# Attention, then a mixture of experts: tokens go by rank to a region per expert, and the experts run as a list of tiles

## The chip, the cores and the metric

The kernel runs on one core of one Trainium2 chip. The core has five engines with queues of their own: PE (TensorE, matrix products; its weight loads are listed apart as PEld), DVE (VectorE), ACT (ScalarE), POOL (GpSimd) and SP (SyncE, here only an issuer of DMAs). All work is in float32. The metric is the device time of one execution in microseconds (us); less is better.

## The reference, cut to what matters

```python
# 1. chunked attention: B=4, H=8, S=768, D=64; chunks of 32, each sees 16 keys to its left, 8 to its right, 8 memory keys
a = exp(scores - max);  a = a / (sum(a) + 1e-9);  out[chunk] = a @ v_full
# 2. x = out as (B, S, 512); each token goes through ONE of E=8 experts
logits = x @ w_gate                      # (B, S, 8)
local_gate = sigmoid(x @ w_local)
for b in range(B):
    for s in range(S):
        fresh = argmax(logits[b, s])
        e = fresh if s == 0 or local_gate[b, s] < 0.5 else e    # else the expert of the token before
        p = softmax(logits[b, s])
        out[b, s] = p[e] * (relu(x[b, s] @ w1[e]) @ w2[e])      # w1: 512x1024, w2: 1024x512 per expert
```

## The kernel before, in words

`attention` works in 32 blocks of 96 queries, 8 to a batch, 4 to a load ("unit": tiles `qt`, `kt`, `vt`, two buffers each). Per block: `scores`, `values` and `logits`. After the 8 blocks of a batch, `route` computes probabilities and experts. `x`, with 8 probabilities behind each token, goes to `x_dram` in token order with one plain DMA per batch on SP's queue. The row `onehot` of each expert and a running count of its tokens (`cum`) stay on chip.

`experts` starts with a sort. From `cum` each token's slot follows, and from the slots, by 32 + 32 small products, the token of each slot (`idx`) and where its result goes (`put`). Slots form tiles of 128, each tile of one expert; 31 tiles are possible, and `bound` holds where each expert's tiles begin. All 31 tiles are then gathered from `x_dram` by indirect DMAs on POOL's queue, turned by PE (`g_ps`) and kept in `xst`. Last comes, for each expert, a loop with a trip count that is known only on the chip (`For_i_unrolled`, two tiles to a pass) over `product`: 32 matmuls into `h_ps`, Relu into `ht`, 8 matmuls into `y_ps`, a scaling into `y`, and an indirect DMA that puts the rows into `out`. The pool `wp` holds the weights of two experts: those of experts 0 and 1 are loaded by SP during attention, those of expert e + 2 after the loop of expert e. A matmul of float32 stands as two instructions in the profile, a transpose as one.

The tile framework writes the waits, and a scheduler sets the order of instructions within straight-line code; it moves nothing past a branch.

Of the kernel before, what the change touches and what calls it, by code (L numbers as in the profile page):

```python
# [15 lines left out]
P = 128  # L16
# [17 lines left out]
XW = D + E                   # a token's row: x, then its probability for each expert  # L34
NTILE = NT // P + E - 1      # tiles of 128 slots when each expert's tokens begin a tile
# [10 lines left out]
@with_exitstack  # L46
def kernel(
    ctx: ExitStack,
    tc: tile.TileContext,
    q: bass.AP,  # L50
    k: bass.AP,
    v: bass.AP,
    mem_k: bass.AP,
    mem_v: bass.AP,
    w_gate: bass.AP,
    w_local: bass.AP,
    w1: bass.AP,
    w2: bass.AP,
    out: bass.AP,
):  # L60
# [25 lines left out]


@with_exitstack
def attention(ctx, tc, q, k, v, mem_k, mem_v, w_gate, w_local, x_dram, ident, onehot, cum, eidx, load_weights):
    """Chunked attention into x_dram; its tokens' experts into onehot, and their ranks (from 1) into cum."""  # L90
# [45 lines left out]
    def mask_of(qb):  # L136
        return masks["first" if qb == 0 else "last" if qb == NQB - 1 else "mid"]

    # e - 8 for each expert; 8 s + 8 for each token s of a batch
# [4 lines left out]
                   allow_small_or_imprecise_dtypes=True)  # L144

# [47 lines left out]
    def route(b, x, lt):  # L193
        """Probabilities into x; the experts of the batch, each carried on by the tokens that its gate keeps."""
# [5 lines left out]
        ex = sm.tile([QB, NQB, E], F32, name="ex")  # L200
        nc.scalar.activation(ex, below, ACT.Exp)
        tot = sm.tile([QB, NQB, 1], F32, name="tot")
        nc.vector.tensor_reduce(tot, ex, axis=AX.X, op=ALU.add)
        nc.vector.tensor_scalar(tot, tot, 1e-9, None, ALU.add)
        nc.vector.reciprocal(tot, tot)
        nc.vector.tensor_tensor(x[:, :, D:XW], ex, tot.to_broadcast([QB, NQB, E]), op=ALU.mult)
        nc.sync.dma_start(x_dram[S * b:S * b + S].rearrange("(j p) c -> p j c", p=QB), x)

# [26 lines left out]
        seg = slice(S * b, S * b + S)  # L235
        nc.vector.tensor_scalar(onehot[:, seg], expert, eidx, None, ALU.is_equal)
# [23 lines left out]
def experts(ctx, tc, x_dram, out, ident, onehot, cum, load_weights, weights):  # L260
# [4 lines left out]
    idx = once.tile([P, NTILE], I32, name="idx")  # L265
    put = once.tile([P, NTILE], I32, name="put")
    bound = once.tile([1, E + 1], I32, name="bound")

    with tc.tile_pool(name="sort", bufs=1) as so, tc.tile_pool(name="sops", bufs=1, space=PSUM) as sops:
        # before[e, m] = 1 where e < m  # L270
        before = so.tile([E, E + 1], F32, name="before")
# [3 lines left out]
        ones = so.tile([E, 1], F32, name="ones")  # L275
        nc.gpsimd.memset(ones, 1.0)
        lo_no = so.tile([QB, P], F32, name="lo_no")
        nc.gpsimd.iota(lo_no, pattern=[[1, P]], base=0, channel_multiplier=0, allow_small_or_imprecise_dtypes=True)
        token = so.tile([QB, NB, 1], F32, name="token")
        nc.gpsimd.iota(token, pattern=[[QB, NB], [0, 1]], base=1, channel_multiplier=1,  # L280
                       allow_small_or_imprecise_dtypes=True)

        # tiles of each expert, and those before its first
        tiles_i = so.tile([E, 1], I32, name="tiles_i")
        nc.vector.tensor_scalar(tiles_i, cum[:, NT - 1:NT], float(P - 1), None, ALU.add)
        nc.vector.tensor_scalar(tiles_i, tiles_i, 7, None, ALU.logical_shift_right)
        tiles = so.tile([E, 1], F32, name="tiles")
        nc.vector.tensor_copy(tiles, tiles_i)
        b_ps = sops.tile([1, E + 1], F32, name="b_ps")
        nc.tensor.matmul(b_ps, lhsT=tiles, rhs=before, start=True, stop=True)  # L290
        nc.vector.tensor_copy(bound, b_ps)
        t_ps = sops.tile([E, 1], F32, name="t_ps")
        nc.tensor.matmul(t_ps, lhsT=before[:, 0:E], rhs=tiles, start=True, stop=True)
        base = so.tile([E, 1], F32, name="base")
        nc.vector.tensor_scalar(base, t_ps, float(P), -1.0, ALU.mult, ALU.add)

        # each token's slot
        nc.vector.scalar_tensor_tensor(cum, cum, base, onehot, ALU.add, ALU.mult)
        s_ps = sops.tile([QB, NB], F32, name="slot_ps")
        for n in range(NB):  # L300
            nc.tensor.matmul(s_ps[:, n:n + 1], lhsT=cum[:, QB * n:QB * n + QB], rhs=ones, start=True, stop=True)
        slot = so.tile([QB, NB], I32, name="slot")
        nc.vector.tensor_copy(slot, s_ps)
# [116 lines left out]
```

## Time and profile before

| what | value |
|---|---|
| time, median of 3 runs | 944.22 us (941.28 to 945.43) |
| span of the profiled execution | 944.2 us |
| PE busy, PEld busy | 757.7 us (80%), 593.7 us (63%) |
| DVE, ACT, POOL busy | 206.0, 169.2, 61.1 us |
| DMA moved | 78.03 MB, 83 GB/s over the span |
| tiles that ran (out of 31) | 27 (DMAs `out_dram<-y,to`) |

The span of the profiled execution is the time of the median run, so that sums made on the trace need no correction. The span falls into three stages: attention up to the last copy of logits (`lt`, ended at 326.1 us), route of the last batch with sort and gathers up to the first product (425.6 us), and the products. PE's busy share is high in all of them, but the trace also shows at which clock PE ran.

### The profile page before, as it was taken

What the parts mean: (1) busy time and instruction counts of PE and PEld (TensorE: products, weight loads), DVE (VectorE), ACT (ScalarE), POOL (GpSimd) and SP (SyncE); (2) the same over time, 40 slices, a digit from 0 to 9 for tenths busy, and PEclk for the clock granted to TensorE, in tenths of its full rate; (3) what the DMA queues carried; (4) which work ended last, traced back from release to release, by engine and by line L of the source; (5) the groups of instructions that cost most, each with busy time, mean ns of one, the idle gap of its engine ahead of it and who ended that gap; (6) DMA issues with size and microseconds to landing.
All of it is one profiled execution on the core that took longest, in us unless ns stands there. A gap on an engine that the chain in (4) does not pass through costs nothing. (4 is left out here: it accounts for less than half of the span.)

```text
span 944.2 us, 12427 instructions
## 1 busy us (share of the span) xinstructions
PE 757.7 (80%) x4144; PEld 593.7 (63%) x4144; DVE 206.0 (22%) x529; ACT 169.2 (18%) x421; POOL 61.1 (6%) x80
## 2 busy tenths in 40 slices
PE   4979889899898745769798968969769779673978
PEld 3877678687777645448565755746547557442655
DVE  3544644555464342330000000000000000000000
ACT  2523234243243000111010101101101011010110
POOL 0000000000000000650000000000000000000000
PEclk8655555555555555558798979979989889895999
DMA  9792331622120010660002040031023000507000
GB/s 238 260 299 72 117 94 28 188 64 59 27 87 1 22 47 3 198 150 11 11 12 82 36 184 21 14 136 58 11 85 127 11 22 12 190 23 270 9 23 2
DMA packets 44458, 78.03 MB, mean 83 GB/s; under 512 B 20269, under 2 KB 20397, under 8 KB 44400
## 3 DMA queue, kind: packets, MB, share of 16 engines
q1 hardware_dynamic: 33728, 54.10, 17.3%
q0 software_dynamic: 4640, 14.55, 5.1%
q10 hardware_dynamic: 6032, 8.61, 3.5%
q8 instruction: 36, 0.59, 0.3%
q14 instruction: 22, 0.18, 0.1%
HBM read 64.57 MB, written 13.47 MB: 83 GB/s over the span
## 5 line engine op out<-in xcount | busy, mean ns | idle before, releaser
L363 PE MATMUL h_ps<-xst,w_sb 128*128 x1728 | 238.2, 301 | 94.4 <-DVE pe L355 41.3
L363 PEld LDWEIGHTS h_ps<-xst,w_sb 128*128 128x128 f32 x1728 | 228.0, 213 | 119.1 <-issue 105.5
L369 PE MATMUL y_ps<-w_sb,ht 128*128 128x512 f32 x432 | 189.9, 592 | 0.0
L369 PEld LDWEIGHTS y_ps<-w_sb,ht 128*128 128x128 f32 x432 | 80.0, 190 | 90.4 <-issue 90.4
L355 DVE COPY pe<-prob 128x1 f32 x27 | 4.2, 154 | 480.8 <-PEq L379 180.1
L174 PE MATMUL o_ps<-vt,pt 128*96 128x65 f32 x512 | 91.5, 354 | 9.4 <-DVE x L178 5.1
L174 PEld LDWEIGHTS o_ps<-vt,pt 128*96 128x96 f32 x512 | 84.6, 267 | 17.4 <-issue 10.4
L161 ACT ACTIVATE s_sb<-s_sb,nmax 96x128 f32<-96x128 f32 x256 | 80.5, 390 | 31.4 <-DVE nmax L159 31.4
L151 PE MATMUL s_ps<-kt,qt 64*96 64x128 f32 x512 | 76.0, 432 | 12.5 <-DMA kt<-in_k_dram 9.1
L366 ACT ACTIVATE ht<-h_ps 128x512 f32<-128x512 f32 x54 | 32.2, 597 | 298.0 <-PE h_ps L363 298.0
L151 PEld LDWEIGHTS s_ps<-kt,qt 64*96 64x96 f32 x512 | 56.6, 265 | 22.2 <-issue 15.1
L168 PE MATMUL pt_ps<-ident,s_sb 96*128 96x96 f32 x256 | 59.2, 374 | 12.7 <-ACT pt L170 9.0
L372 POOL DMA_INDIRECT out_dram<-y,to x27 | 26.6, 984 | 496.6 <-ACT y L371 431.2
L168 PEld LDWEIGHTS pt_ps<-ident,s_sb 96*128 96x128 f32 x256 | 43.2, 224 | 23.1 <-ACT pt L170 13.8
L170 ACT COPY pt<-pt_ps 128x384 f32<-128x384 f32 x64 | 30.4, 477 | 139.1 <-PE o_ps L174 98.6
L371 ACT ACTIVATE y<-y_ps,pe 128x512 f32<-128x512 f32 x27 | 18.6, 687 | 169.4 <-PE y_ps L369 169.4
L345 PE MATMUL g_ps<-ident,xs 128*128 128x128 f32 x124 | 33.3, 428 | 16.8 <-DMA xs<-x_dram,idx 12.8
L190 PEld LDWEIGHTS l_ps<-wg,xt 128*96 128x96 f32 x256 | 42.2, 265 | 2.2 <-DVE xt L187 0.9
L190 PE MATMUL l_ps<-wg,xt 128*96 128x9 f32 x256 | 41.5, 292 | 0.7 <-DVE xt L187 0.7
L345 PEld LDWEIGHTS g_ps<-ident,xs 128*128 128x128 f32 x124 | 22.2, 217 | 27.6 <-issue 16.7
L159 DVE TENSOR_REDUCE nmax<-s_sb 96x8 f32<-96x1024 f32 x32 | 38.3, 1198 | 0.1
L339 POOL DMA_INDIRECT xs<-x_dram,idx x31 | 29.5, 952 | 51.6 <-issue 41.6
(86 smaller groups left out, 308.8 us busy)
## 6 DMA issues: line engine op xcount, KB each, us to landing
w_sb<-in_w_dram SPq DMA_DIRECT2D x16, 2048.0 KB
vt<-in_v_dram ACTq DMA_DIRECT2D x32, 243.8 KB
kt<-in_k_dram SPq DMA_DIRECT2D x32, 240.0 KB
x_dram<-x SPq DMA_DIRECT2D x4, 1560.0 KB
qt<-in_q_dram SPq DMA_DIRECT2D x8, 768.0 KB
vt<-in_mem_v_dram ACTq DMA_DIRECT2D x32, 16.2 KB
xs<-x_dram,idx POOLq DMA_INDIRECT x31
out_dram<-y,to POOLq DMA_INDIRECT x27
```

The source lines that it names most:

```text
L151: nc.tensor.matmul(s_ps[:, u, a], lhsT=qt[h, a, QB * j:QB * j + QB], rhs=kt[h, j, a], start=True, stop=True)
L159: nc.vector.tensor_reduce(nmax, s_sb, axis=AX.X, op=ALU.max, negate=True)
L161: nc.scalar.activation(s_sb[:, i], s_sb[:, i], ACT.Exp, bias=nmax[:, i:i + 1])
L168: nc.tensor.transpose(pt_ps[:, a], s_sb[:, HP * u + a], identity=ident[:QB, :QB])
L170: nc.scalar.copy(pt, pt_ps)
L174: nc.tensor.matmul(o_ps[:, a], lhsT=pt[:, a], rhs=vt[:, j, VW * h:VW * h + VW], start=True, stop=True)
L190: nc.tensor.matmul(l_ps, lhsT=xt[:, kk], rhs=wg[:, kk], start=(kk == 0), stop=(kk == DK - 1))
L339: nc.gpsimd.indirect_dma_start(out=xs, out_offset=None, in_=x_dram[:, :], in_offset=bass.IndirectOffsetOnAxis(ap=idx[:, i:i + 1], axis=0))
L345: nc.tensor.transpose(g_ps[:, kk], xs[:, P * kk:P * kk + P], identity=ident)
L363: nc.tensor.matmul(h_ps[:, m], lhsT=w1_sb[:, kk, P * (g + m):P * (g + m) + P], rhs=xst[:, bass.ds(i, 1), kk, :].rearrange("p o n -> p (o n)"),
L366: nc.scalar.activation(ht[:, g:g + 4], h_ps, ACT.Relu)
L369: nc.tensor.matmul(y_ps, lhsT=ht[:, m], rhs=w2_sb[:, m], start=(m == 0), stop=(m == FK - 1))
```

## The change

1. `route` ends otherwise. `count` is carried over batches; each token's row in DRAM is `4096 * expert + rank`, computed by one more DVE operation and 8 matmuls (`r_ps`). A row of `x` is now 514 words: 512 of x, the probability of its own expert, the token's number. The 8 blocks of the batch go to these rows by 8 indirect DMAs on POOL's queue (L263 of the kernel after).
2. The sort is gone. A plan for 31 tiles (expert, first row, last row of each) is made from the 8 counts by some 25 small DVE operations.
3. The loops are gone. 24 tiles (3072 tokens / 128, the least there can be) stand in straight-line code, and 7 more each inside an `If(total > i)`, nested. A tile's own loads of `w1` and `w2` (4.2 MB, four buffers each, the expert read from `table`), its gather and its transposes stand in the tile.
4. No weights are loaded during attention. The host lays `w1` and `w2` out so that a partition's share is one run of 16 KB (before: runs of 4 KB and 2 KB).

```diff
-XW = D + E                   # a token's row: x, then its probability for each expert
+XW = D + 2
+SURE = NT // P
+NTILE = SURE + E - 1
+REGION = 4096
+WBUF = 4
@@ route
-        nc.sync.dma_start(x_dram[S * b:S * b + S].rearrange("(j p) c -> p j c", p=QB), x)
...
-        nc.vector.tensor_tensor_scan(cum[:, seg], onehot[:, seg], onehot[:, seg],
-                                     cum[:, S * b - 1:S * b] if b else 0.0, ALU.add, ALU.max)
+        nc.vector.tensor_tensor_scan(rank, onehot, onehot, count, ALU.add, ALU.max)
+        nc.vector.tensor_copy(count, rank[:, S - 1:S])
+        nc.vector.scalar_tensor_tensor(rank, rank, region, onehot, ALU.add, ALU.mult)
+        r_ps = xps.tile([QB, NQB], F32, name="r_ps", tag="xps")
+        for n in range(NQB):
+            nc.tensor.matmul(r_ps[:, n:n + 1], lhsT=rank[:, QB * n:QB * n + QB], rhs=ones, start=True, stop=True)
+        row = sm.tile([QB, NQB], I32, name="row")
+        nc.vector.tensor_copy(row, r_ps)
...
+        nc.vector.tensor_tensor(x[:, :, D:D + 1], mine, tot, op=ALU.mult)
+        nc.vector.tensor_copy(x[:, :, D + 1:XW], token[:, NQB * b:NQB * b + NQB])
+        for n in range(NQB):
+            nc.gpsimd.indirect_dma_start(
+                out=x_dram[:, :], out_offset=bass.IndirectOffsetOnAxis(ap=row[:, n:n + 1], axis=0),
+                in_=x[:, n].bitcast(I32), in_offset=None)
...
-        if 2 <= n < 4:
-            load_weights(n - 2)
@@ experts
-    for i in range(NTILE):
-        xs = gp.tile([P, XW], F32, name="xs")
...
+    def load(i):
+        e = nc.values_load(table[:, i:i + 1], engines=[SP], min_val=0, max_val=E - 1,
+                           skip_runtime_bounds_check_because="made from counts of tokens")
+        xs = gp.tile([P, XW], F32, name="xs")
+        nc.gpsimd.indirect_dma_start(
+            out=xs.bitcast(I32), out_offset=None, in_=x_dram[:, :],
+            in_offset=bass.IndirectOffsetOnAxis(ap=rows[:, i:i + 1], axis=0))
+        w1_sb = wp.tile([P, DK, F], F32, name="w1_sb")
+        nc.sync.dma_start(w1_sb, w1[bass.ds(e, 1)].rearrange("o p k f -> p (o k) f"))
+        w2_sb = wp.tile([P, FK, D], F32, name="w2_sb")
+        nc.sync.dma_start(w2_sb, w2[bass.ds(e, 1)].rearrange("o p m d -> p (o m) d"))
+        return xs, w1_sb, w2_sb
+
+    def turned(i, xs):
         g_ps = gps.tile([P, DK, P], F32, name="g_ps")
         for kk in range(DK):
             nc.tensor.transpose(g_ps[:, kk], xs[:, P * kk:P * kk + P], identity=ident)
...
+        xt = gp.tile([P, DK, P], F32, name="xt")
+        nc.vector.tensor_copy(xt, g_ps)
+        to = hp.tile([P, 1], I32, name="to")
+        nc.vector.tensor_tensor(to, xs[:, D + 1:XW], past[:, i:i + 1], op=ALU.add)
+        return xt, to
...
-    for e in range(E):
-        a, z = (nc.values_load(bound[0:1, n:n + 1], min_val=0, max_val=NTILE,
-                               skip_runtime_bounds_check_because="a count of tiles") for n in (e, e + 1))
-        tc.For_i_unrolled(a, z, 1, lambda i: product(e, i), max_unroll=2)
-        if e + 2 < E:
-            load_weights(e + 2)
+    for i in range(SURE):
+        xs, w1_sb, w2_sb = load(i)
+        xt, to = turned(i, xs)
+        product(xs, xt, to, w1_sb, w2_sb)
+
+    for i in range(SURE, NTILE):
+        ctx.enter_context(tc.If(total > i))
+        xs, w1_sb, w2_sb = load(i)
+        xt, to = turned(i, xs)
+        product(xs, xt, to, w1_sb, w2_sb)
```

The first place is POOL's queue from the last two batches of attention into the tiles. Before, it held there only copies of memory keys (`kt<-memk`), constants and all 31 gathers:

```order
L109 COPY kt<-memk 128x16x8 x7
L272 MEMSET before 8x9
L276 MEMSET ones 8x1
L278 IOTA lo_no 96x128
L273 AFFINE_SELECT before<-before 8x9
L280 IOTA token 96x32
L339 DMA xs<-x_dram,idx 128x520 x31
L377 TENSOR_LOAD bound x2
```

After, with the semaphores that each instruction waits for (DMASW0 to DMASW7 count POOL's own DMAs as they land), the 8 scatters of the last batch and what follows:

```order
L263 DMA x_dram<-x,row 32768x514 [waits DMASW7_49,DVE_49]
L263 DMA x_dram<-x,row 32768x514 [waits DMASW0_49]
L263 DMA x_dram<-x,row 32768x514 [waits DMASW1_49]
L263 DMA x_dram<-x,row 32768x514 [waits DMASW2_49]
L263 DMA x_dram<-x,row 32768x514 [waits DMASW3_49]
L263 DMA x_dram<-x,row 32768x514 [waits DMASW4_49]
L263 DMA x_dram<-x,row 32768x514 [waits DMASW5_49]
L263 DMA x_dram<-x,row 32768x514 [waits DMASW6_49]
L366 DMA xs<-x_dram,rows 128x514 [waits DVE_49,DMASW7_49,PE_49,Pool_49]
L366 DMA xs<-x_dram,rows 128x514 x3
L399 DMA out_dram<-y,to 3072x512 [waits DVE_49,Activation_49]
L366 DMA xs<-x_dram,rows 128x514 [waits DMASW0_49,PE_49]
```

Each scatter waits for the one before it to land, the first gather for the last scatter, and later gathers alternate with the writes of results, four tiles ahead of them. The scatters of batches 0 to 2 stand in the same way between the copies `kt<-memk` of later units.

The second place is PE at the start of the experts. Before, all 124 transposes, then loops with registers and branches:

```order
L227 MATMUL c_ps<-ident,code 8x96 x8
L290 MATMUL b_ps<-before,tiles 1x9
L293 MATMUL t_ps<-tiles,before 8x1
L301 MATMUL slot_ps<-ones,cum 96x1 x32
L323 MATMUL p_ps<-hi_is,lo_is 128x31 x32
L345 MATMUL g_ps<-ident,xs 128x128 x124
L377 TENSOR_LOAD bound x2
L379 REGISTER_ALU x2
L379 COMPARE_AND_BRANCH
```

After, the transposes of four tiles, then products back to back, with the transposes of two tiles between every two products:

```order
L222 MATMUL c_ps<-ident,code 8x96 x8
L240 MATMUL r_ps<-ones,rank 96x1 x8
L319 MATMUL b_ps<-before,tiles 128x9
L320 MATMUL b_ps<-ident,count 128x8
L378 MATMUL g_ps<-ident,xs 128x128 x16
L391 MATMUL h_ps<-xt,w_sb 128x128 x32
L396 MATMUL y_ps<-w_sb,ht 128x512 x8
L391 MATMUL h_ps<-xt,w_sb 128x128 x32
```

The products moved up to where the 62 sorting matmuls and most of the transposes stood. The third place is POOL where the tiles under `If` begin; before there is nothing of the kind. After:

```order
L399 DMA out_dram<-y,to 3072x512 x4
L360 TENSOR_LOAD total_i
_compat.py:109 COMPARE_AND_BRANCH
L366 DMA xs<-x_dram,rows 128x514
L399 DMA out_dram<-y,to 3072x512
_compat.py:109 COMPARE_AND_BRANCH
L366 DMA xs<-x_dram,rows 128x514
```

The gather of each such tile stands behind the branch, and the branch behind the result of the tile before; the four tiles of lead are gone there. SP's loads of weights stand behind SP's own branches alone, and wait for nothing but their buffer.

## Rows read from the trace of the kernel before

**Rows 1.** Windows of the three stages: busy us by engine, PE clock, DMA share, GB/s.
```profile
0.00:326.20 326.20, 275.70 (x1712) 239.67 (x1712) 162.76 (x393) 109.35 (x324) 3.25 (x17) 0.55 0.38 111
326.20:425.60 99.40, 60.69 (x273) 48.21 (x273) 35.35 (x83) 9.05 (x16) 31.29 (x36) 0.50 0.37 100
425.60:944.20 518.60, 421.34 (x2160) 305.80 (x2160) 7.88 (x54) 50.80 (x81) 26.58 (x27) 0.90 0.17 61
```

**Rows 2.** Timeline of PE in the products: start, length, instruction, idle time ahead.
```profile
425.59 10.35 PE L363 MATMUL h_ps<-xst,w_sb 128*128 x64 [1.65 <-issue]
...
592.31 8.98 PE L363 MATMUL h_ps<-xst,w_sb 128*128 x64 [5.27 <-PEq L379]
...
865.63 13.04 PE L363 MATMUL h_ps<-xst,w_sb 128*128 x64 [21.56 <-DVE pe L355]
...
885.38 7.31 PE L363 MATMUL h_ps<-xst,w_sb 128*128 x64
892.52 7.03 PE L369 MATMUL y_ps<-w_sb,ht 128*128 128x512 f32 x16
899.39 7.31 PE L363 MATMUL h_ps<-xst,w_sb 128*128 x64
...
932.70 7.03 PE L369 MATMUL y_ps<-w_sb,ht 128*128 128x512 f32 x16
```

**Rows 3.** Timeline of the last route and sort, and of the first gathers.
```profile
325.98 0.16 DVE L191 COPY lt<-l_ps 96x9 f32<-96x9 f32 x1 [1.54 <-PE l_ps L190]
...
335.34 1.80 DVE L237 TENSOR_TENSOR_SCAN cum<-onehot,cum 8x768 f32<-8x768 f32 x1
...
338.44 3.40 DVE L298 SCALAR_TENSOR_TENSOR cum<-cum,base,onehot 8x3072 f32<-8x3072 f32 x1
...
341.90 10.39 PE L301 MATMUL slot_ps<-ones,cum 8*96 8x1 f32 x64 [3.89 <-DVE cum L298]
...
375.49 1.13 POOL L339 DMA_INDIRECT xs<-x_dram,idx  x1 [38.02 <-issue]
...
379.21 1.08 PE L345 MATMUL g_ps<-ident,xs 128*128 128x128 f32 x4 [5.35 <-DMA xs<-x_dram,idx]
...
380.56 0.68 DVE L349 COPY xst<-g_ps 128x512 f32<-128x512 f32 x1
```

**Rows 4.** Chain that ended last: pieces spent until an indirect write had landed.
```profile
886.54 2.62 DMA out_dram<-y,to
...
900.55 3.16 DMA out_dram<-y,to
...
914.57 2.73 DMA out_dram<-y,to
```

**Rows 5.** Windows in which weights were moved, and the window 50 to 75 us.
```profile
852.00:860.00 8.00, 0.00 (x0) 0.00 (x0) 0.00 (x0) 0.00 (x0) 0.00 (x0) 0.50 1.04 398
...
872.00:874.00 2.00, 2.00 (x12) 1.49 (x11) 0.00 (x0) 0.60 (x1) 0.00 (x0) 1.00 0.36 136
...
50.00:75.00 25.00, 19.82 (x122) 17.67 (x121) 12.10 (x27) 7.17 (x21) 0.00 (x0) 0.50 0.81 251
```

**Rows 6.** Timeline around one tile's end and the load of `w2` at 865.42.
```profile
865.42 0.37 SPq L81 DMA_DIRECT2D w_sb<-in_w_dram  x1
...
885.58 0.69 ACT L371 ACTIVATE y<-y_ps,pe 128x512 f32<-128x512 f32 x1 [6.27 <-PE y_ps L369]
...
886.54 0.98 POOL L372 DMA_INDIRECT out_dram<-y,to  x1 [40.49 <-DVE pe L355]
```

**Rows 7.** Timelines in attention: SP, PE, POOL and DVE.
```profile
52.78 0.39 SPq L80 DMA_DIRECT2D w_sb<-in_w_dram  x1
...
65.02 1.55 PE L174 MATMUL o_ps<-vt,pt 128*96 128x65 f32 x8 [4.27 <-ACT pt L170]
...
128.63 0.29 POOL L109 COPY kt<-memk 128x128 f32<-128x128 f32 x1 [40.80 <-PE s_ps L151]
...
155.16 0.16 DVE L176 TENSOR_SCALAR rinv<-o_ps 96x4 f32<-96x4 f32 x1 [3.48 <-PE o_ps L174]
```

More of the change, by code (lines that the diff above doesn't have):

```diff
@@ L33 @@
 NT = B * S
[L34 to L35 removed]
+XW = D + 2
+SURE = NT // P
+NTILE = SURE + E - 1
+REGION = 4096
+SHIFT = 12
 FAR = 4096
+WBUF = 4
 GATE = -1.5 * 2.0 ** -23
@@ new lines, in route @@
+        nc.vector.tensor_copy(row, r_ps)
+        ex = sm.tile([QB, NQB, E], F32, name="ex")
+        nc.scalar.activation(ex, below, ACT.Exp)
+        tot = sm.tile([QB, NQB, 1], F32, name="tot")
+        nc.vector.tensor_reduce(tot, ex, axis=AX.X, op=ALU.add)
+        nc.vector.tensor_scalar(tot, tot, 1e-9, None, ALU.add)
+        nc.vector.reciprocal(tot, tot)
+        mine_i = sm.tile([QB, NQB], I32, name="mine_i")
+        nc.vector.tensor_scalar(mine_i, row, SHIFT, None, ALU.logical_shift_right)
@@ L259, in experts @@
 @with_exitstack
-def experts(ctx, tc, x_dram, out, ident, onehot, cum, load_weights, weights):
+def experts(ctx, tc, x_dram, out, ident, count, w1, w2):
     nc = tc.nc
     once = ctx.enter_context(tc.tile_pool(name="eonce", bufs=1))
[L265 to L271, printed above, removed]
+    wp = ctx.enter_context(tc.tile_pool(name="wp", bufs=WBUF))
+    gp = ctx.enter_context(tc.tile_pool(name="gp", bufs=4))
+    hp = ctx.enter_context(tc.tile_pool(name="hp", bufs=2))
+    table = once.tile([1, NTILE], I32, name="table")
+    total_i = once.tile([1, 1], I32, name="total_i")
+    rows = once.tile([P, NTILE], I32, name="rows")
+    past = once.tile([P, NTILE], F32, name="past")
+    with tc.tile_pool(name="plan", bufs=1) as pl, tc.tile_pool(name="plps", bufs=1, space=PSUM) as plps:
+        before = pl.tile([E, E + 1], F32, name="before")
         nc.gpsimd.memset(before, 1.0)
@@ L286, in experts @@
+        tiles_i = pl.tile([E, 1], I32, name="tiles_i")
+        nc.vector.tensor_scalar(tiles_i, count, float(P - 1), None, ALU.add)
         nc.vector.tensor_scalar(tiles_i, tiles_i, 7, None, ALU.logical_shift_right)
-        tiles = so.tile([E, 1], F32, name="tiles")
+        tiles = pl.tile([E, 1], F32, name="tiles")
         nc.vector.tensor_copy(tiles, tiles_i)
-        b_ps = sops.tile([1, E + 1], F32, name="b_ps")
-        nc.tensor.matmul(b_ps, lhsT=tiles, rhs=before, start=True, stop=True)
@@ L291, in experts @@
[L291 to L301, printed above, removed]
@@ L320, in experts @@
-        nc.vector.tensor_tensor(hi_is, hi_is, token.to_broadcast([QB, NB, NTILE]), op=ALU.mult)
-        p_ps = sops.tile([P, NTILE], F32, name="p_ps")
-        for n in range(NB):
-            nc.tensor.matmul(p_ps, lhsT=lo_is[:, n], rhs=hi_is[:, n], start=(n == 0), stop=(n == NB - 1))
-        nc.vector.tensor_scalar(idx, p_ps, -1.0, 0.0, ALU.add, ALU.max)
-        empty = so.tile([P, NTILE], F32, name="empty")
-        nc.vector.tensor_scalar(empty, p_ps, 0.0, float(FAR), ALU.is_equal, ALU.mult)
@@ L327, in experts @@
-        nc.vector.scalar_tensor_tensor(put, p_ps, -1.0, empty, ALU.add, ALU.add)
-    xst = once.tile([P, NTILE, DK, P], F32, name="xst")
-    prob = once.tile([P, NTILE, E], F32, name="prob")
-    gp = ctx.enter_context(tc.tile_pool(name="gp", bufs=4))
-    hp = ctx.enter_context(tc.tile_pool(name="hp", bufs=2))
+        b_ps = plps.tile([P, 2 * E + 1], F32, name="b_ps")
+        nc.tensor.matmul(b_ps[:, 0:E + 1], lhsT=tiles.to_broadcast([E, P]), rhs=before, start=True, stop=True)
+        nc.tensor.matmul(b_ps[:, E + 1:2 * E + 1], lhsT=count.to_broadcast([E, P]), rhs=ident[:E, :E],
+                         start=True, stop=True)
@@ L345, in experts, with product @@
             nc.tensor.transpose(g_ps[:, kk], xs[:, P * kk:P * kk + P], identity=ident)
[L346 to L355 removed]
+        xt = gp.tile([P, DK, P], F32, name="xt")
+        nc.vector.tensor_copy(xt, g_ps)
         to = hp.tile([P, 1], I32, name="to")
[L357 removed]
+        nc.vector.tensor_tensor(to, xs[:, D + 1:XW], past[:, i:i + 1], op=ALU.add)
+        return xt, to
+    def product(xs, xt, to, w1_sb, w2_sb):
         ht = hp.tile([P, FK, P], F32, name="ht")
```

135 lines of the change are left out of this document (67 added, 68 removed).

## The prediction

> **What bounds the kernel now.** I read the windows by stage first, then the timeline of PE in the last stage, then the chain of waits, then the DMA windows. The three stages [rows 1] take 326.2, 99.4 and 518.6 us. In the first, PE is busy 276 of 326 us at a granted clock of 0.55, so mostly at 1.2 GHz: attention is bound by PE at its lower level. In the middle stage nothing of the reference's products is computed: it is the last route, the sort, 31 gathers and 124 transposes, one after the other. In the last, PE is busy 421 of 519 us at 0.90. What a product costs when nothing disturbs it is seen in the second tile of a pair: 7.14 us from its first `h_ps` matmul to its first `y_ps` matmul (885.38 to 892.52) and 6.87 us from there to the next tile (899.39), 14.01 us at 2.4 GHz [rows 2]. 27 tiles would be 378 us; the stage takes 518.6. The other 140 us are at the loops' ends: PE sits idle for 5 to 8 us, once 21.56 us, and then `h_ps` takes 8.98, 10.35 or 13.04 us instead of 7.31, since PE comes back at 1.2 GHz [rows 2]. So there are two things to win: most of 99.4 us in the middle and most of 140 us in the products.
>
> **Attention, up to the last logits.** Removed: 8.4 MB of weights in the first 75 us. PE's idle time of 4.27 us ahead of 65.02, behind the weights issued from 52.78 on, goes: ACT, on which PE waits there, issues the loads of `vt` on its own queue, and these stand behind weights [rows 7]. Added on PE, for batches 0 to 2: 8 matmuls `r_ps`, a quarter of the 64 instructions that took 10.39 us [rows 3], 2.6 us a batch at 1.2 GHz, and PE is the bound here. Before `r_ps` PE waits in order for DVE's longer chain; no row has that wait. Its lower bound is nothing (PE has 10 us of other products ahead of `r_ps`), its upper bound the 8 us from the `onehot` scan to the slots' first product, 335.34 to 341.90 and some; I take 1.5 us, nearer the lower, since DVE idles half of this stage. So -4.3 + 3 x 4.1 = +8.0, and the last `lt` stands at 334.1 instead of 326.1.
>
> The scatters of batches 0 to 2 I cost at nothing. Their cover is POOL's idle time. What could end it is the buffer of `x`: batch 2 writes the buffer of batch 0, and DVE waits for all 8 scatters of that batch. Six of them stand behind the copy `kt<-memk` of unit 5, which ran at 128.63; 6 x 2.84 us (below) is 17 us, so until 146, or 149 if the two ahead of the copy delay it. The first scaling of batch 2 ran at 155.16 [rows 7]. That is 6 to 9 us of slack; without it every us more is a us on DVE, and PE behind it.
>
> **Route of the last batch.** From `lt` to the end of the running count it stays 11.0 us (326.14 to 337.14). New are the operation over 8 x 768, a quarter of 3.40 us, `r_ps` with 2.6 us [rows 3], and some 15 small DVE operations until the last column of `x` is written, 0.2 us each by the row of `lt` (0.16 and its gap), four of them over 248 to 279 elements, taken twice: 4.0 us. Together 18.4 us; `x` is ready at 352.5. The plan's other operations and the register load of the first expert lie beside the scatters.
>
> **The scatters.** By the order, each of the 8 waits for the one before to land, since all write one tensor. From issue until an indirect write of similar size had landed took 2.62, 3.16 and 2.73 us [rows 4], mean 2.84: 8 x 2.84 = 22.7 us, between 21 and 25. Nothing covers this: POOL's gathers are behind it in its queue, and SP's first weight load waits for all that attention's memory held, `x` too. So gather and weights start at 375.2.
>
> **Start of the tiles.** PE's first product stands behind 16 transposes, so behind four gathers. Undisturbed, the first gather took 3.7 us until its transposes began (375.49 to 379.21); three more issues at 1.25 us and the last transposes bring 9.3 us, the lower bound [rows 3]. The weights alone took 7.3 us: issued at 865.42, the DMA share runs out at about 872.7 [rows 5, 6]. But both start together. If the gathers' 1.05 MB landed only after the whole tile 0 (4.2 MB), at 398 GB/s [rows 5], that is 13.2 us, plus some 2 us ahead and 1.5 behind: 17 us, the upper bound. I take 13, the middle. The Trainium skill (DMA: Bandwidth & Descriptors, Queues, rings and completion order) says that each DMA engine takes turns between the queues by whole packets; with runs of 16 KB against rows of 2 KB that speaks for the upper bound, and the sum would be 4 us higher. The same page (Anatomy of one DMA) gives a fixed 2.0 us and 436 GB/s for a DMA of POOL; the scatters would by that be an estimated 2.45 us each, 19.6 instead of 22.7. Against that stand the three rows; they decide.
>
> First product: 375.2 + 13 = 388.2, where before it was 425.6.
>
> **24 tiles in a row.** 24 x 14.01 = 336.2. The transposes of 20 of them now stand between products: 1.08 us at 1.2 GHz [rows 3], so 0.54 at 2.4, and a part of the copy's 0.68 us is waited for, 0.2 a tile: 14.8. Cold start of the first `h_ps`: 10.35 against 7.31 [rows 2], 3.0. Sum 354.0, until 742.2. Hidden is the stream of weights. A tile needs 4.2 MB, and with gather and result 4.72 MB in 14.75 us, 320 GB/s; the windows with nothing but weights ran at 398, at a DMA share of 1.04 [rows 5]. Four buffers let it run ahead.
>
> **3 tiles under `If`.** The gather stands behind the result of the tile before, so there is a gap: `y` on ACT 0.9 us, its issue on POOL 1.2 [rows 6], gather 3.7, transposes 1.1 and copy 0.7 [rows 3], 7.6 us. Then PE is back at 1.2 GHz: 10.4 us for `h_ps`, the middle one of the three rows, and 6.9 for `y_ps` [rows 2]. 24.9 each, 74.7, and 1 us for registers: until 818. Bounds: 44 if the gap did not show, 90 if each `h_ps` took 13.04 and the branch cost 2 us.
>
> **End.** The last `y_ps` ended at 939.73 [rows 2], the span at 944.2: 4.5 us more, as before. Sum 822.
>
> **The rivals.** (a) PE's clock in attention: the mean of 0.55 [rows 1] says that PE runs at 2.4 GHz now and then; without weights in the way a denser PE may hold it longer. If a third of the 276 busy us ran at twice the clock, 46 us would go: 776. Against it: the stage's later parts have no weights before either, and stay at 0.5. (b) Costs of seams: 8 us more per batch in attention, the upper bounds of scatters, start and `If` together give 822 + 19 + 3 + 4 + 15: 863. For it: four sizes that no row has. (c) The other side: the weights' stream becomes the bound. With 27 x 4.2 MB, it moves 113 MB where 33.5 were moved before. Each tile of 24 then takes 4.72 MB over the rate. At the 251 GB/s of the window 50 to 75 us [rows 5] it would be 18.8 us, 822 + 24 x 4.05 = 919; below 238 GB/s (19.8 us) the kernel is not faster, at 230 it takes 960. For it: that window mixes several queues, as the tiles will. Against it: its small rows of `kt` (480 B) have no part in the tiles, and the stream of weights beside a busy PE reached 398. (d) The change moves the time nowhere, because PE was busy 80% already: 944. Against it: 99 + 140 us above are seen idle or at half clock.
>
> **How the numbers follow.** Forecast 0.68, (a) 0.09, (b) 0.17, (c) 0.05, of that 0.03 above 948.9, (d) 0.01. A measurement of this kernel can tell about 0.5% from no change. So faster 0.96, same 0.01, slower 0.03. The forecast's own range is 800 to 845; the range that leaves out no more than 2 in 10 reaches half into (a) and to (b): 784 to 864.
>
> **What would show it.** Right: the first `h_ps` between 380 and 396; POOL's last 8 scatters spaced by 2.6 to 3.2 us; tiles 0 to 23 every 14 to 15 us at a clock near 1.0; three gaps of 7 to 9 us at the end; DMA near 320 GB/s among the tiles. Wrong: gaps ahead of `h_ps` waiting for `w_sb` (c), attention ending much before 330 (a) or after 345 (b), or gaps in front of transposes among the first 24 tiles, which would mean that POOL's queue does not keep its lead.

## The result and the profile after

The changed kernel takes 839.51 us (median of 4 runs, 836.76 to 847.82) against 944.12 us (941.28 to 945.43): a ratio of 0.8906, 95% interval 0.8849 to 0.8962. The forecast was 822 in a range of 784 to 864, so the side, the range and the forecast's own range (800 to 845) hold; the time is 17.5 us longer than the forecast. The profiled execution is the longest of the four, 847.8 us with a span of 846.1; below, a second profile of the same kernel with a span of 841.1 stands beside it. One of the four executions of the kernel with short runs below took 1020.42 us at a mean granted clock of 0.597 and is left out of its range.

The windows of the changed kernel, cut where the prediction cut its sum (columns as in [rows 1]): attention, route, scatters, start of the tiles, 24 tiles, three tiles under `If`, end.

```profile
0.00:339.97 339.97, 293.42 (x1760) 254.82 (x1760) 168.98 (x421) 109.36 (x324) 26.97 (x49) 0.53 0.29 82
339.97:358.27 18.30, 6.44 (x36) 5.33 (x36) 11.95 (x39) 0.26 (x1) 0.00 (x1) 0.50 0.00 0
358.27:386.41 28.14, 0.00 (x0) 0.00 (x0) 2.28 (x11) 0.00 (x0) 7.35 (x9) 0.50 0.19 56
386.41:406.68 20.27, 4.17 (x17) 3.06 (x18) 2.30 (x5) 0.00 (x0) 3.81 (x4) 0.50 0.97 393
406.68:759.70 353.02, 349.56 (x2001) 254.70 (x2000) 17.08 (x43) 44.48 (x71) 42.70 (x43) 0.99 0.86 333
759.70:832.50 72.80, 52.47 (x253) 38.62 (x252) 2.55 (x6) 5.64 (x9) 5.94 (x6) 0.84 0.07 22
832.50:846.00 13.50, 0.00 (x0) 0.00 (x0) 0.00 (x0) 0.69 (x1) 1.00 (x1) 0.68 0.01 2
```

Against [rows 1]: the middle stage of 99.4 us became 18.3 + 28.1 + 20.3 = 66.7, the products' 518.6 became 353.0 + 72.8 + 13.5 = 439.3, and attention's 326.2 became 340.0. That is -32.7 - 79.3 + 13.8 = -98.2, the difference of the spans but for rounding. In the fifth row PE is busy 99% at 2.4 GHz: the loops' ends of [rows 2] are gone. Everything that took longer than forecast lies in the other rows.

POOL's timeline of the changed kernel at the scatters and the first gathers (start, length, instruction, idle time ahead and what ended it):

```profile
358.27 0.92 POOL L263 DMA_INDIRECT x_dram<-x,row  x1 [41.57 <-DVE x L260]
361.78 0.92 POOL L263 DMA_INDIRECT x_dram<-x,row  x1 [2.59 <-DMA x_dram<-x,row]
...
382.31 0.92 POOL L263 DMA_INDIRECT x_dram<-x,row  x1 [2.46 <-DMA x_dram<-x,row]
386.41 0.97 POOL L366 DMA_INDIRECT xs<-x_dram,rows  x1 [3.18 <-DMA x_dram<-x,row]
...
390.20 0.94 POOL L366 DMA_INDIRECT xs<-x_dram,rows  x1 [0.31 <-issue]
```

PE's timeline of the same kernel behind it:

```profile
395.38 1.09 PE L378 MATMUL g_ps<-ident,xs 128*128 128x128 f32 x4 [39.49 <-DMA xs<-x_dram,rows]
398.83 1.12 PE L378 MATMUL g_ps<-ident,xs 128*128 128x128 f32 x4 [2.36 <-DMA xs<-x_dram,rows]
402.05 1.09 PE L378 MATMUL g_ps<-ident,xs 128*128 128x128 f32 x4 [2.11 <-DMA xs<-x_dram,rows]
405.80 1.08 PE L378 MATMUL g_ps<-ident,xs 128*128 128x128 f32 x4 [2.65 <-DMA xs<-x_dram,rows]
406.68 9.17 PE L391 MATMUL h_ps<-xt,w_sb 128*128 128x128 f32 x64
```

POOL is done with the gathers' issue at 391.1, yet the transposes that wait for them start one every 3.2 to 3.8 us, the last at 405.8. PE's timeline at the first tile under `If`, where 5.8 us of waiting and a cold `h_ps` are seen:

```profile
752.85 7.03 PE L396 MATMUL y_ps<-w_sb,ht 128*128 128x512 f32 x16
765.71 1.08 PE L378 MATMUL g_ps<-ident,xs 128*128 128x128 f32 x4 [5.82 <-DMA xs<-x_dram,rows]
767.58 9.69 PE L391 MATMUL h_ps<-xt,w_sb 128*128 128x128 f32 x64 [0.78 <-DVE xt L380]
```

### The profile page after: what moved, and what is told of

Same layout as the page of the kernel before. It is cut to its first block, busy times and chain, and to the rows that moved or that the text cites. A ratio compares the mean times of both kernels' runs of the same rounds, so it can differ in the third digit from the quotient of the medians.

```text
span 846.1 us, 10132 instructions
## 1 busy us (share of the span) xinstructions
PE 706.1 (83%) x4064; PEld 556.5 (66%) x4064; DVE 205.1 (24%) x522; ACT 160.4 (19%) x406; POOL 87.8 (10%) x111
## 4 chain that ended last, share of the span: by engine, by line
PE 61%; issue 13%; DMA 13%; DVE 8%; ACT 1%; POOL 1%; ACTq 0%; POOLq 0%; DVEq 0%
PE h_ps L391 16%; PE y_ps L396 15%; PE o_ps L178 9%; PE s_ps L155 7%; DMA out_dram<-y,to 5%; PE pt_ps L172 5%; PE l_ps L194 4%; DMA xs<-x_dram,rows 3%; PE xt_ps L189 3%; DMA x_dram<-x,row 3%; PE c_ps L222 1%; PE r_ps L240 1%; DVE s_sb L159 1%; DMA vt<-in_v_dram 1%; DVE x L182 1%
## 5 line engine op out<-in xcount | busy, mean ns | idle before, releaser
L391 PEld LDWEIGHTS h_ps<-xt,w_sb 128*128 128x128 f32 x1728 | 204.2, 198 | 15.6 <-DVE xt L380 8.2
L391 PE MATMUL h_ps<-xt,w_sb 128*128 128x128 f32 x1728 | 206.7, 282 | 5.8 <-DVE xt L380 5.0
L178 PE MATMUL o_ps<-vt,pt 128*96 128x65 f32 x512 | 95.1, 364 | 5.8 <-DVE x L182 4.4
L178 PEld LDWEIGHTS o_ps<-vt,pt 128*96 128x96 f32 x512 | 88.2, 277 | 13.9 <-issue 10.6
L382 DVE TENSOR_TENSOR to<-xs,past 128x1 int32<-128x1 f32 x27 | 4.3, 159 | 370.0 <-DMA out_dram<-y,to 224.8
L378 PE MATMUL g_ps<-ident,xs 128*128 128x128 f32 x108 | 18.0, 313 | 64.6 <-DMA xs<-x_dram,rows 64.6
L399 POOL DMA_INDIRECT out_dram<-y,to x27 | 27.3, 1013 | 386.7 <-ACT y L398 352.7
L378 PEld LDWEIGHTS g_ps<-ident,xs 128*128 128x128 f32 x108 | 14.4, 161 | 73.5 <-issue 64.1
L263 POOL DMA_INDIRECT x_dram<-x,row x32 | 29.6, 925 | 247.3 <-DVE x L260 171.6
L398 ACT ACTIVATE y<-y_ps,xs 128x512 f32<-128x512 f32 x27 | 18.6, 688 | 170.9 <-PE y_ps L396 164.6
L194 PEld LDWEIGHTS l_ps<-wg,xt 128*96 128x96 f32 x256 | 44.8, 280 | 1.8 <-DVE xt L191 0.9
```

Source lines behind the costliest of these rows:

```text
L178: nc.tensor.matmul(o_ps[:, a], lhsT=pt[:, a], rhs=vt[:, j, VW * h:VW * h + VW], start=True, stop=True)
L194: nc.tensor.matmul(l_ps, lhsT=xt[:, kk], rhs=wg[:, kk], start=(kk == 0), stop=(kk == DK - 1))
L263: nc.gpsimd.indirect_dma_start(out=x_dram[:, :], out_offset=bass.IndirectOffsetOnAxis(ap=row[:, n:n + 1], axis=0), in_=x[:, n].bitcast(I32 ...
L378: nc.tensor.transpose(g_ps[:, kk], xs[:, P * kk:P * kk + P], identity=ident)
L391: nc.tensor.matmul(h_ps[:, m], lhsT=w1_sb[:, kk, P * (g + m):P * (g + m) + P], rhs=xt[:, kk], start=(kk == 0), stop=(kk == DK - 1))
```

## The experiments

Theory: the gain is the sort's stage and the loops' ends; what it falls short by is four terms, each with a mechanism of its own: scatters that wait for one another, gathers that take turns with 16 KB packets of weights, `If`s, and an attention that follows PE's granted clock. Rivals: these costs belong to POOL's queue in any form, or to the bytes, or to attention's added work. "The kernel run again" below is the changed kernel of e0_again.

**The same kernel again (e0_again), and the kernel before again (e11_before_again).**

> The changed kernel once more, nothing edited, as the yardstick for the runs beside it and for a second profile of attention. Theory: attention's end follows the granted clock of the execution and nothing else, so the last lt moves by several us from the 339.8 of the first profile where the mean clock differs, while route (18.3), scatters (28.0), start of the tiles (20.5), 24 tiles (353.0), three If tiles (72.6) and the end (13.6) come again within 1 us each. Rival: attention's 5.9 us over the forecast are fixed work on DVE and POOL; then the last lt stands at 339 to 341 again whatever the clock. Time 837 to 848.

> The kernel before once more, nothing edited, for a second profile of its attention. If attention's end is set by how long PE was granted 2.4 GHz, then the last lt differs from 325.98 by some us where the mean clock over the first 325 us differs from 0.55, in the same sense as between the profiles of the changed kernel (328.6 to 339.8 there); if it stands at 325 to 327 again with another clock, the changed kernel's longer attention is its own work.

840.65 us (837.78 to 843.44) for the one, 948.3 (one run) for the other, beside 946 to 947 for the median of the kernel before in these comparisons. The clock of attention is read from the window 20 to 325 us, third number from the end. The kernel before, in the execution of [rows 1]:

```profile
20.00:325.00 305.00, 267.58 (x1646) 232.50 (x1646) 156.31 (x372) 107.53 (x322) 1.76 (x6) 0.53 0.35 103
```

The kernel before again:

```profile
20.00:325.00 305.00, 269.55 (x1627) 234.61 (x1626) 154.64 (x366) 107.39 (x322) 1.76 (x6) 0.51 0.34 103
```

The changed kernel, in the execution shown above:

```profile
20.00:325.00 305.00, 275.21 (x1637) 238.49 (x1637) 156.90 (x383) 106.34 (x319) 24.00 (x30) 0.50 0.27 75
```

The changed kernel again:

```profile
20.00:325.00 305.00, 275.06 (x1650) 237.97 (x1650) 157.74 (x387) 107.05 (x321) 23.98 (x30) 0.51 0.26 75
```

The last `lt` came at 325.98, 331.88, 339.81 and 337.40. So it moves by 6 us in the kernel before too, and the second and fourth, both at 0.51, are to be compared: +5.5 us. Other runs below with the same attention bear this out: the kernel before had 331.98 at 0.51 (e5_before_no_early_weights), the changed one 337.3 at 0.51 (e2_gather_ahead, e10_18_tiles), 339.6 at 0.50 (e14_two_weight_buffers) and 328.6 at 0.53 (e1_no_if). The one pair at 0.53, 325.98 and 328.6, differs by 2.6 us only, so a mean clock of two digits leaves some us open. (The profile of e3_short_runs has no clock on record ahead of 399 us.) Two rows of PE's timeline split this; both begin with the 73rd matmul instruction of `o_ps`. The kernel before again:

```profile
69.50 1.54 PE L174 MATMUL o_ps<-vt,pt 128*96 128x65 f32 x8 [4.95 <-ACT pt L170]
```

The changed kernel again:

```profile
65.42 1.52 PE L178 MATMUL o_ps<-vt,pt 128*96 128x65 f32 x8 [0.68 <-ACT pt L174]
```

The stall shrank from 4.95 to 0.68 and the product came 4.1 us earlier; from there to the last `lt` it took 262.4 before and 272.0 after, 9.6 us more for three routes. Of these, 8.1 are the matmuls `r_ps`, which stand in each of the three batches without a wait ahead of them; the first, in the execution shown above:

```profile
118.49 2.71 PE L240 MATMUL r_ps<-ones,rank 8*96 8x1 f32 x16
```

Both theories have a share: a fixed part of +5.5, and a profile of before that had PE at 2.4 GHz for longer. Why one execution is granted it for longer than another is open. The other stages came again at 18.3, 27.1, 19.7, 352.6, 72.1 and 13.7 us.

**The kernel before without early weights (e5_before_no_early_weights).** The two calls `load_weights(0)`, `load_weights(1)` were moved behind `attention`.

> The kernel before with one edit: the first two experts' weights are issued behind attention instead of at 13 to 75 us. It asks for the -4.3 us of the prediction by itself. Theory: PE's stall of 4.27 us ahead of 65 us goes, and the last lt comes some 4 us earlier than the 325.98 of the profile before, near 322, where the granted clock has the same pattern; the weights, 8.4 MB, hide beside the sort: 940 for 944. Rival: what the stall costs PE gives back at once, since PE comes out of it at 2.4 GHz; without it PE stands at 1.2 GHz from 20 us on, as in the profile of the changed kernel, and lt comes at 326 to 335: no gain, 943 to 952.

945.72 us (937.11 to 948.12), ratio 0.9977, interval 0.9945 to 1.0009. It tells nothing of the weights: SP's timeline has them at the old place, 19.98 to 57.27 us, since the scheduler had put them there again, and the stall of 5.04 us stands. So that the stall goes with the early weights is argued from [rows 7] and not shown. The rival's reason isn't seen either: behind the stall of [rows 7] the granted clock stayed at 0.50 from 66 to 97 us. It is a third profile of the kernel before, its last `lt` at 331.98.

**No `If` (e1_no_if).**

```diff
-    for i in range(SURE):
...
-        ctx.enter_context(tc.If(total > i))
+    for i in range(27):
```

> All 27 tiles in one straight line, no If and no register load of the total (the input of this case has 27 tiles, so nothing is left out). Theory: the If alone makes the three gaps of 9 to 10 us and the cold h_ps behind them, and the arms that are skipped make the 13.6 us of the end; so the last three tiles take 3 x 14.7 = 44 instead of 72.6 and the end some 4.5 instead of 13.6: 37 to 38 us faster than the changed kernel, near 802. Rival 1: the long end belongs to POOL's indirect DMAs in any form; then the end stays at 13 and only 28 us go (811). Rival 2: the gaps come from POOL's order (gather behind the result of the tile before) also in a straight line; then the first 24 tiles would show them too, and nothing moves.

808.70 us (804.59 to 812.54): 32 less than the kernel run again. 27 is this input's number of tiles, so this kernel doesn't hold for others. The last three tiles begin and end with

```profile
747.77 1.04 PE L377 MATMUL g_ps<-ident,xs 128*128 128x128 f32 x8
...
785.92 7.03 PE L395 MATMUL y_ps<-w_sb,ht 128*128 128x512 f32 x16
```

They took 45.1 us (747.77 to 792.9) in place of 72.1: the theory's part on the tiles. The end took 10.0 us in place of 13.7: between theory and rival 1. Of the 9 us that I put down to skipped arms, 3.7 are theirs.

**18 tiles (e10_18_tiles), and what the end is.** As above with `range(18)`, so it leaves out the results of the last nine tiles.

> The straight line without If cut to 18 tiles: the last nine tiles' rows are left out of the result. It asks what the end consists of: the last DRAIN of POOL took 2.7 us in the kernel before with 58 indirect transfers, 7.1 in the changed one and 8.3 without If, with 86. If it grows with the number of transfers, 68 give some 4.3 us; if it is a matter of the form of the kernel, 7 to 8.5 again. Time: 808.7 - 9 x 14.73 = 676, or 672 with the shorter end. Among the tiles nothing should change: 14.0 for the first three, 15.5 for each pair's one with transposes ahead.

677.54 us (one run), span 675.8. The views leave out POOL's housekeeping; the trace's own records of it around the last issue, in start and length (DRAIN is the last long record on POOL; INC_SWDGE_SEM stands there only in kernels with `If`):

```
changed    833.54 1.00 DMA_INDIRECT   836.09 1.90 INC_SWDGE_SEM   838.18 7.09 DRAIN
no If      794.00 0.98 DMA_INDIRECT                               793.76 8.32 DRAIN
18 tiles   668.38 0.98 DMA_INDIRECT                               668.15 6.86 DRAIN
before     940.73 0.98 DMA_INDIRECT                               940.65 2.70 DRAIN
```

Where the DRAIN starts last, it takes 7.09 us with 86 transfers of POOL (changed) and, in kernels below, 7.42 with 90 and 7.75 with 94. Where the last issue stands inside it, 7.10 us pass from the issue's end to the DRAIN's with 86 transfers (no `If`) and 5.65 with 68. That is 0.08 us for each transfer throughout, whether the added ones are gathers of 128 rows (90) or scatters of 96 (94), and it is not the landing: the last result landed 2.2 to 2.3 us after its issue. In the changed kernel 3.6 us lie between the last issue and the DRAIN: a wait for that landing, 1.90 us of INC_SWDGE_SEM and branches. That is what the skipped arms cost. The expected 4.3 us was too low since I drew the line through the kernel before, which drains at the end of its loops too (2.98 us at 663.02, for one).

**Gathers and transposes ahead (e2_gather_ahead).**

```diff
+    more = []
+    for i in range(SURE, NTILE):
+        xs, xt, to = ...               # one buffer each, in `once`
+        gathered(i, xs)
+        turned(i, xs, xt, to)
+        more.append((xs, xt, to))
     for i in range(SURE, NTILE):
         ctx.enter_context(tc.If(total > i))
-        xs, w1_sb, w2_sb = load(i)
-        xt, to = turned(i, xs)
-        product(xs, xt, to, w1_sb, w2_sb)
+        w1_sb, w2_sb = load(i)
+        product(*more[i - SURE], w1_sb, w2_sb)
```

> The gathers and transposes of the seven possible further tiles are made ahead of the Ifs, for all seven and into buffers of their own; only weights and products stay under an If. Theory: the gap in front of each If tile is the chain result, gather, transposes, copy; with it gone PE waits only for the branch and goes on at 2.4 GHz: three tiles in 44 to 48 instead of 72.6, plus 7 x 0.7 = 5 for the transposes ahead: 20 to 24 us faster than the changed kernel, near 818. With three POOL transfers fewer in each skipped arm, the end may be up to a few us shorter. Rival: the weights, which are issued inside the If, are what is waited for; then a gap of 5 us and more ahead of h_ps stays, and the gain is under 10 us.

818.32 us (815.43 to 820.86), 22.3 less. PE's timeline at the first two tiles under `If`:

```profile
762.45 7.40 PE L389 MATMUL h_ps<-more_xt,w_sb 128*128 128x128 f32 x64 [0.65 <-PE g_ps L379]
769.69 7.03 PE L394 MATMUL y_ps<-w_sb,ht 128*128 128x512 f32 x16
776.56 7.31 PE L389 MATMUL h_ps<-more_xt,w_sb 128*128 128x128 f32 x64
```

A tile under an `If` is as fast as any other, 14.1 us: the branch costs nothing that PE waits for, and the gap was the chain from result to gather to transposes.

**Short runs (e3_short_runs).**

```diff
-        nc.sync.dma_start(w1_sb, w1[bass.ds(e, 1)].rearrange("o p k f -> p (o k) f"))
+        nc.sync.dma_start(w1_sb, w1[bass.ds(e, 1)].rearrange("o (k p) f -> p (o k) f", p=P))
```

and `w2` alike, with the host's layout of before.

> The weights are read in runs of 4 KB and 2 KB, as the kernel before read them, instead of 16 KB; the same bytes and the same products. Theory: at the start of the tiles the gathers of x take turns packet by packet with the weights, and a 16 KB packet makes each gather 3.3 us; with short packets the transposes of the first four tiles follow each other in 1.3 to 1.6 us, and the first h_ps comes 10 to 13 us after the first gather's issue instead of 20.5: 8 to 10 us faster than the changed kernel, near 831. Rival: the gathers wait for bytes of the weights issued ahead of them whatever the packets; then the start stays at 20 us and the time at 837 to 848. Second rival: short runs cost rate; the DMA share among the tiles is 0.80 to 0.87 now, and if it passes 1.0, gaps ahead of h_ps appear and the kernel is slower by some us a tile.

836.91 us (834.09 to 837.21), 3.7 less than the kernel run again where I expected 8 to 10. The intervals of the two ratios overlap (0.8789 to 0.8888 and 0.8837 to 0.8929), so the time alone shows little; attention's last `lt`, at 339.76 here and 337.40 there, hides a part. By stages it is plain: POOL's first gather was issued at 386.08, and PE's timeline goes on

```profile
393.30 1.08 PE L378 MATMUL g_ps<-ident,xs 128*128 128x128 f32 x4 [37.45 <-DMA xs<-x_dram,rows]
394.68 1.12 PE L378 MATMUL g_ps<-ident,xs 128*128 128x128 f32 x4 [0.30 <-DMA xs<-x_dram,rows]
396.31 1.97 PE L378 MATMUL g_ps<-ident,xs 128*128 128x128 f32 x8 [0.51 <-DMA xs<-x_dram,rows]
398.06 8.02 PE L391 MATMUL h_ps<-xt,w_sb 128*128 128x128 f32 x64
```

12.0 us in place of 19.7 and 20.3, and gathers 1.4 to 1.6 us apart, about POOL's rate of issue (1.26). Both rivals fall: the bytes are the same, and the 24 tiles take 352.9 us as before. The packet records of the two traces show the turns themselves. In the changed kernel 256 packets of 4112 B (two rows each) of the four gathers start within 13.4 us, and among them 285 packets of weights, each of 16384 B: nearly one for one. A gather's packet takes 0.16 us, a weight's 0.61 (medians). With short runs the same 256 are through in 5.7 us, among 362 packets of weights of 4 and 2 KB. So the theory of turns holds. The Trainium skill (DMA: Bandwidth & Descriptors, Queues, rings and completion order) says that an engine switches between queues at packet boundaries only; the two starts and the packet counts agree with it.

**Two weight buffers (e14_two_weight_buffers).** `WBUF = 2`.

> Two buffers for w1 and two for w2 instead of four each. Theory: the stream of weights is hidden with room to spare; a buffer is free 21 us before it is needed again, a load of 2.1 MB takes 5 us at 425 GB/s, so the tiles stay at 14.0 and 15.5 us and the time at 837 to 848. Rival, the one that would make the weights the bound: running ahead by four tiles is what hides the stream; with two, h_ps or y_ps waits for w_sb by 1 us or more in each tile: 865 or above.

852.76 us (849.94 to 857.55): slower than I expected, but not by the rival. The window of the 24 tiles:

```profile
410.16:762.96 352.80, 349.34 (x2001) 254.51 (x2000) 17.08 (x43) 44.46 (x71) 42.87 (x43) 1.00 0.83 314
```

352.8 us as with four buffers. The 12 us lie elsewhere. From first scatter (356.67) to first gather it took 33.6 us: POOL's constants of the plan, made early in the changed kernel, stand behind the scatters here, and the first gather waits 5.92 us for DVE's `rows`. And two of the three gaps under `If` grew to 8.80 and 9.35 us, since a load of `w2`, issued at 763.15 as its buffer came free, runs beside the gather issued at 765.48; the third, with no load beside it, stayed at 6.27. From POOL's timeline, then PE's:

```profile
390.22 0.99 POOL L366 DMA_INDIRECT xs<-x_dram,rows  x1 [5.92 <-DVE rows L353]
...
771.92 1.09 PE L378 MATMUL g_ps<-ident,xs 128*128 128x128 f32 x4 [8.80 <-DMA xs<-x_dram,rows]
...
824.29 1.09 PE L378 MATMUL g_ps<-ident,xs 128*128 128x128 f32 x4 [6.27 <-DMA xs<-x_dram,rows]
```

**Each scatter twice (e7_scatter_twice).** A second copy goes to `x2_dram`.

> Each of the last eight scatters is issued a second time, into another DRAM tensor that nobody reads. Theory: what a scatter waits for is that the one before into the same tensor has landed; the second copy is free to go in that wait, so the eight take 28 to 36 us together, not 56. Rival: POOL's queue takes one indirect transfer at a time, or the rows' bytes are the limit; then the stretch doubles to some 56 us and the span grows by 28. At the end: with 94 transfers of POOL in place of 86, the last DRAIN of POOL takes 8 us or more instead of 7.1 if it grows with their number (58 in the kernel before: 2.7), and 7.1 again if it doesn't.

842.9 us (one run), span 841.2. POOL's timeline, L264 being the scatters into `x_dram` and L268 the second copies:

```profile
355.22 0.92 POOL L264 DMA_INDIRECT x_dram<-x,row  x1 [42.26 <-DVE x L261]
356.44 0.92 POOL L268 DMA_INDIRECT x_dram<-x,row  x1 [0.30 <-issue]
358.69 0.92 POOL L264 DMA_INDIRECT x_dram<-x,row  x1 [1.33 <-DMA x_dram<-x,row]
...
382.53 0.98 POOL L371 DMA_INDIRECT xs<-x_dram,rows  x1 [1.77 <-DMA x_dram<-x,row]
```

16 scatters took 27.3 us, 8 took 27.1 to 28.1. The rival falls: it is the wait for the landing, not POOL's queue or the bytes.

**Route by half batches (e8_route_half).**

```diff
-        if half == 1:
-            route(b, x, lt)
+        route(b, half, x, lt, latest)     # 4 blocks; run = scan from latest, the last column of the run before
```

> The route is made after each half batch (four blocks) instead of each batch, the running maximum being carried over; so only four scatters stand behind the last logits. Theory: each exposed scatter costs 3.5 us, its issue and the wait until it has landed, so the stretch of the scatters falls from 28.0 to 14, and the route itself, with operations half as long, from 18.3 to some 14: 18 us less between the last lt and the first gather; against it stand four more routes in attention, about 1 us each: some 14 us faster than the changed kernel run again, near 826. Rival: PE waits in order at r_ps for DVE's chain twice as often, up to 8 us each; then attention ends 30 us later and the kernel is slower, near 854.

834.35 us (825.69 to 839.03), ratio 0.8789 (0.8730 to 0.8847) where the kernel run again had 0.8883 (0.8837 to 0.8929). That is 6 us by the medians and 9 by the ratios, with intervals that still touch; 14 were expected. The profile is of the longest execution, 839.03. Its last `lt` stands at 350.36, and POOL's timeline has

```profile
362.46 0.92 POOL L265 DMA_INDIRECT x_dram<-x,row  x1 [11.59 <-DVE x L262]
...
376.73 0.97 POOL L367 DMA_INDIRECT xs<-x_dram,rows  x1 [3.11 <-DMA x_dram<-x,row]
```

26.2 us from logits to gather in place of 45.4, as the theory had it and a little more. But attention ends 13 us later than in the changed kernel's second profile, 3.2 us for each route added, not 1; the two kernels below, with the same route, end it at 349.3 and 351.6. This is the rival's mechanism at a lower price: PE now waits for DVE ahead of six of the seven `r_ps` groups in attention, 15.1 us in all, where the changed kernel has no such wait. The first of them:

```profile
72.41 1.41 PE L242 MATMUL r_ps<-ones,rank 8*96 8x1 f32 x8 [2.72 <-DVE rinv L182]
```

**All three (e9_ahead_short_half), and with late gathers (e16_all_late_gathers).** The second adds `late = rows + (to & 0)` at tile 14 as the indices of the seven gathers.

> Three edits together: gathers and transposes of the further tiles ahead of the Ifs, weights in short runs, route by half batches. If the three stretches are separate the gains add: 22 (measured alone, between 820 and 841 in the medians) + 8.5 (start of the tiles 20.5 to 12.0) + 14 = 44 us less than the changed kernel run again, near 796. Rival: the gathers ahead, eleven in a row at the start, take the short runs' gain back, or the half route costs more in attention than it saves; then 805 to 815.

> The three edits together, with one more: the gathers of the seven further tiles depend on the indices of tile 14, so that they can't go at the start of the tiles. Beside them tile 0 waited 3.54 us for its w2 and its products took 1.8 us longer; 1.8 MB in rows ahead of the weights are 4.3 us at 425 GB/s. Theory: that goes, and 4 to 5 us of the time, near 802.5 for 807. Rival: tile 0's w2 is late because the weights were issued 8 us later than the first gathers could use, with or without the seven; then tile 0 waits as before and the time is 807.

807.19 us (798.77 to 811.96), ratio 0.8488 (0.8421 to 0.8556), the fastest kernel of the study that holds for any split of tokens. The expected 796 was not reached and the rival's 805 to 815 is right, for two reasons: the half route gives less than the 14 us put in, as above, and tile 0 takes 21.1 us, since it waits for weights that stand beside eleven gathers:

```profile
399.95 8.80 PE L395 MATMUL y_ps<-w_sb,ht 128*128 128x512 f32 x16 [3.54 <-DMA w_sb<-in_w_dram]
```

With late gathers that wait is gone (tile 0 takes 14.7 us), but the time is 817.06 (815.46 to 818.94), above both the 802.5 and the 807 expected. DVE's timeline shows why:

```profile
605.85 0.16 DVE L385 TENSOR_TENSOR more_to<-more_xs,past 128x1 int32<-128x1 f32 x1 [1.00 <-DMA more_xs<-x_dram,late]
605.93 1.28 DVE L384 COPY xt<-g_ps 128x512 f32<-128x512 f32 x2
```

And PE's:

```profile
606.67 8.91 PE L393 MATMUL h_ps<-xt,w_sb 128*128 128x128 f32 x64 [11.42 <-DVE xt L384]
```

Seven small `more_to`, each waiting for its gather, stand on DVE ahead of the copy `xt` that the next product needs: a stall of 3.5 us became one of 11.4.

## Why the prediction was right, and where its sizes were off

| term | forecast | changed | changed again | off |
|---|---|---|---|---|
| attention until `lt` | 334.1 | 340.0 | 337.6 | +3.5 to +5.9 |
| route | 18.4 | 18.3 | 18.3 | -0.1 |
| scatters | 22.7 | 28.1 | 27.1 | +4.4 to +5.4 |
| start of the tiles | 13 | 20.3 | 19.7 | +6.7 to +7.3 |
| 24 tiles | 354.0 | 353.0 | 352.6 | -1.0 to -1.4 |
| three tiles under `If` | 75.7 | 72.8 | 72.1 | -2.9 to -3.6 |
| end | 4.5 | 13.5 | 13.7 | +9.0 to +9.2 |

The gain came where it was forecast; four sizes were too low, by 24 to 28 us together, and two that were too high gave back 4 to 5, so a little of the nearness is luck. Two of the signs named in advance did not come: the first `h_ps` stood at 406.7 and 402.7 and not before 396, and the scatters were spaced by 3.4 to 3.5 us in the mean and not by 2.6 to 3.2.

- **The gain** is where it was said to be: tiles at 14.0 us back to back, with transposes between. The stream of weights is hidden: 333 GB/s at a share of 0.86 among the tiles, 393 GB/s at the start, and 24 tiles are as long with two buffers. Rival (c) falls, and so does (a): attention had no higher clock after, 0.50 to 0.53 in the profiles with the same attention against 0.51 to 0.53 before.
- **End**, +9: I took "4.5 us more, as before". The shown rows of before had nothing of POOL's DRAIN. It takes 0.08 us for each of 86 transfers, 5.5 us more than the 1.6 that stood behind the last issue before; the skipped arms are the other 3.7 us. The line through kernels with 68 to 94 transfers shows it; why a transfer costs that is open.
- **Start**, +7: the upper bound of 17 was passed. It supposed that the gathers' 1.05 MB land behind tile 0's 4.2 MB. (The 7.3 us given for "the weights alone" are those of one load of 2.1 MB, half of what tile 0 needs.) At 393 GB/s some 8.0 MB moved in the 20.3 us, so more than one tile's weights went ahead. The cause, turns by packets, was weighed in the prediction, and I took the middle. The short runs and the packet records show it.
- **Scatters**, +5: the mechanism is right (e7_scatter_twice), the price not. 2.84 us was the time from issue to landing of a result's write; these land after 3.2 us by the profile's list of DMA issues, and the next issue starts some 0.2 to 0.3 us after that: 3.4 to 3.5 in the mean. The 2.45 us estimated from the Trainium skill (DMA: Bandwidth & Descriptors, Anatomy of one DMA) was further off; the trace decides.
- **Attention**: the removed stall was worth 4.1 us (forecast 4.3), three routes 9.6 (forecast 12.3), net +5.5 for +8.0. `r_ps` took 2.7 us a batch as forecast (2.6); the 1.5 us of waiting ahead of it, for which no row was given, did not come there, and 1.5 us of the 9.6 stay unexplained. The rest is the base: 326.1 came from an execution with a mean clock of 0.53 from 20 us on, and two others of the same kernel end attention at 332. In the scatters of batches 0 to 2 nothing was found that PE or DVE waits for, but no run took them away alone.
- **`If`**, -3: the gap is 5.8 to 6.4 us of waiting for the gather; `h_ps` took 9.2 to 9.7 and not 10.4. Rival (b), upper bounds everywhere, had two of its four sizes: scatters above their 25 and start above its 17. Without those of attention and `If` its 863 was not reached.

## What to carry to other kernels

Price a chain of dependent DMAs by the spacing of their issues, and ask of each wait whether another tensor or queue would lift it. Here each small gather that started beside a stream of weights paid for that stream's 16 KB packets, so ask for long runs only where nothing small is waited for. Work that is moved out of an exposed stretch is not free where it goes: half routes took 19 us off that stretch and put 13 into attention. And look in the raw records at what an engine still does after its last listed instruction, and take a second profile before attributing a few us in a stage where PE's clock changes.

## What the runs showed of the hardware that was not expected

- From its last issue to the end of its DRAIN, or in the DRAIN alone where that starts later, POOL takes 5.65, 7.09, 7.42 and 7.75 us behind 68, 86, 90 and 94 indirect transfers.
- The same straight-line attention ends between 328.6 us (e1_no_if, mean clock 0.53 from 20 us on) and 339.8 us (0.50); PE's granted clock stands at 1.2 GHz for most of it although PE is busy nine tenths of the time.
- Four gathers of 0.26 MB beside weights in 16 KB runs reach PE 3.2 to 3.8 us apart, beside runs of 4 and 2 KB 1.4 to 1.6 us; in the first case packets of the two queues start nearly one for one (256 and 285).
